# Loading the last fifth of the query weights through GpSimd, and finishing a head between the next products, in a one-token attention and ReGLU kernel

## The chip, the cores and the metric

The kernel runs on one core of a Trainium2 chip. The metric is device time in microseconds (us) of one execution, the median of several runs; lower is better. The core's engines are TensorE (PE in the profile; PEld are its weight loads), VectorE (DVE), ScalarE (ACT), GpSimd (POOL) and SyncE (SP). Sixteen DMA engines, which the core's queues share, bring data from the device's memory into the on-chip memory. A queue belongs to the engine that issues on it.

## The reference

One token `x` (640 values) goes through a layer norm, attention with 32 heads of 192 columns over a cache of 8192 positions, and a gated ReGLU block, with a residual sum after each. Everything is float32.

```python
def _A_ref(x, k_cache, v_cache, wq, wo):          # B = Sq = 1, D = 640, H = 32, Sk = 8192, Dh = 192
    q = (x @ wq).reshape(B, Sq, H, Dh).transpose(0, 2, 1, 3)
    scores = jnp.einsum("bhqd,bhkd->bhqk", q, k_cache) * (Dh ** -0.5)
    p = _softmax(scores, axis=-1)
    o = jnp.einsum("bhqk,bhkd->bhqd", p, v_cache)
    return o.transpose(0, 2, 1, 3).reshape(B, Sq, H * Dh) @ wo

def _B_ref(x, W_gate, W_up, W_down):              # F = 1536
    gate = jnp.einsum("bsd,df->bsf", x, W_gate)
    up = jnp.einsum("bsd,df->bsf", x, W_up)
    gate = gate * (gate > 0)
    return jnp.einsum("bsf,fd->bsd", gate * up, W_down)

h = x + _A_ref(_layernorm(x), A_k_cache, A_v_cache, A_wq, A_wo)
h2 = h + _B_ref(_layernorm(h), B_W_gate, B_W_up, B_W_down)
```

The two caches are 201 MB each, `wq` and `wo` 15.7 MB each, and the three matrices of the ReGLU block 3.9 MB each. Each value is used once.

## The kernel before

**Start.** ACT issues the load of `x` as the tile `xT` (L65: partition p holds the five values 5p to 5p+4, 20 bytes for each of 128 partitions) and once more as one row, `xrow` (L66). SP issues the query weights `wq` (L74) in three loads: two of 6144 KB, in which a partition gets two neighbouring rows (49,152 bytes in one piece), and one of 3072 KB with the fifth row of each partition. Each load fills one of the three buffers of the pool `kv`. VectorE and TensorE work out mean and variance of `xT` (L127 to L145) and write the normalized token `xn`. In between stand four small products on TensorE that add `xrow` to the accumulator `acc` (L150). Then come the products of `xn` and `wq` (L160), one weight row of a partition after the other, so buffer by buffer; each is 12 products, which the profile shows as 24 rows. ScalarE copies the result to `q4`, from which `query(h)` (L169) spreads one head's query over all partitions.

**Buffers set the order of the loads.** All key and value loads of SP (`load_kv`, L82; 6144 KB each) go through the same three buffers in turn. The first key load, K0, takes the buffer of the first `wq` load, so SP issues it when the products of the weight rows j = 0 and 1 are done; then SP issues `wo` of the first four heads (L91), K1 into the second buffer and V0 into the third. SP's instructions are in program order: whatever stands behind a waiting load waits too. After that the sequence is K2, V1, K3, V2 and so on, each load waiting until the third load before it has been used up.

**A head.** In `scores_and_softmax` VectorE multiplies the keys of head h+1 with the query in four parts (L187), GpSimd folds the two halves of each product (L188), and VectorE sums them to scores (L193). Between the four multiplications run the softmax steps of head h: the maximum (L198, L200, L203), the exponential on ScalarE (L205 to L210), the sum and its reciprocal (L212, L215). `values_of` then multiplies the probabilities of head h with its values, 32 products on TensorE (L229, 64 rows), and ScalarE scales the result into `ob` (L232).

**Finishing a head.** Once the scores of head h+1 are summed, `finish` treats the head before h: `to_columns` selects the result's diagonal by small products (L244) and VectorE transposes it into `oT` (L247); after the last head of a group of four (two for the last two groups), `output_of` multiplies `oT` by that group's `wo` into `acc` (L253).

**End.** The last value load comes in five parts. Then the ReGLU weights are loaded into the same buffers, the layer norm of `acc` is worked out, and products with up, gate and down weights (L327, L344) give the output.

`keep` fixes the order of the instructions that it wraps; the others are placed by the framework as they become ready.

Of the kernel before, what the change touches and what calls it, by code (L numbers as in the profile page):

```python
# [7 lines left out]
F32 = mybir.dt.float32  # L8
# [6 lines left out]
def kernel(  # L15
# [24 lines left out]
    QB = 512  # L40
    NQB = HPQ * DH // QB
    DG = D // NQ
    FG = F // NQ
# [18 lines left out]

    xT = const.tile([P, DJ], F32, name="xT")
    xrow = const.tile([1, D], F32, name="xrow")
    nc.scalar.dma_start(xT, x[0, 0].rearrange("(p j) -> p j", p=P))  # L65
    nc.scalar.dma_start(xrow, x[0])  # L66


    wq_v = wq.rearrange("(p j) n -> p j n", p=P)
    wq_ts = []  # L70
    for j in range(0, DJ, 2):
        n = min(2, DJ - j)
        t3 = kv.tile([P, 2 * TW], F32, name="kv_t").rearrange("p (j n) -> p j n", n=TW)[:, 0:n, :]
        nc.sync.dma_start(t3, wq_v[:, j:j + n, :])  # L74
# [98 lines left out]

    keep = tc.keep_in_program_order

    def scores_and_softmax(q, kt, sc_prev):


        steps = softmax_steps(sc_prev) if sc_prev is not None else iter(())
        sc = small.tile([P, NS], F32, name="sc") if kt is not None else None  # L180
        parts = []
        if kt is not None:
            k3 = kt.rearrange("p (r d) -> p r d", d=DH)
            parts = [(i0, k3[:, i0:i0 + SUB, :]) for i0 in range(0, NS, SUB)]
        res = None
        for i0, ks in parts:
            keep(nc.vector.tensor_mul(ks, ks, q[:, None, :].to_broadcast([P, SUB, DH])))  # L187
            nc.gpsimd.tensor_add(ks[:, :, 0:HD], ks[:, :, 0:HD], ks[:, :, HD:DH])  # L188
# [5 lines left out]
        return sc, res  # L194

    def softmax_steps(sc):
# [3 lines left out]
        nc.tensor.transpose(pt[0:1, 0:P], mp, ident)  # L200
        yield None
# [11 lines left out]
        yield None  # L213
        rl = small.tile([P, 1], F32, name="rl")
        keep(nc.vector.reciprocal(rl, pl[:, 0:1]))  # L215
        yield p, rl

# [7 lines left out]
    def values_of(h, p, rl, vt):  # L225
        po = pos[h % 2]
        for i in range(NP):
            g = i % NQ
            nc.tensor.matmul(po[g * Q:g * Q + 2, :], p[:, 2 * i:2 * i + 2],  # L229
                             vt[:, 2 * i * DH:(2 * i + 2) * DH], start=(i < NQ), stop=(i >= NP - NQ))  # L230
        ob = small.tile([P, 2 * DH], F32, name="ob")
        nc.scalar.activation(ob, po, AF.Copy, scale=rl)  # L232
        return ob

    def to_columns(h, ob, oT):

        gi, i = group_of[h]
        U = NQ // len(GROUPS[gi])
        W = DH // U
        pt = ps_s.tile([P, 512], F32, name="ps_small")  # L240
        for u in range(U):
            q0 = (i * U + u) * Q
            for k in range(2):
                nc.tensor.matmul(pt[q0:q0 + Q, 0:W], par[:, k, :], ob[:, k * DH + u * W:k * DH + (u + 1) * W],  # L244
                                 start=(k == 0), stop=(k == 1))
        s = slice(i * U * Q, (i + 1) * U * Q)
        keep(nc.vector.transpose(oT[s], pt[s, 0:W].rearrange("p (c j) -> p j c", c=Q)))  # L247

    def output_of(oT, wo_t, s, last):
        J = wo_t.shape[1]  # L250
        for j in range(J):
            for g in range(NQ):
                nc.tensor.matmul(acc[g * Q:(g + 1) * Q, :], oT[s, j, :], wo_t[s, j, g * DG:(g + 1) * DG],  # L253
                                 start=False, stop=(last and j == J - 1))

    def finish(h, ob, oT, wo_t):
        i, n = group_of[h][1], len(GROUPS[group_of[h][0]])
        to_columns(h, ob, oT)
        if n == 2 and h >= H - 2:
            output_of(oT, wo_t, slice(i * 64, (i + 1) * 64), h == H - 1)  # L260
        elif i == n - 1:
            output_of(oT, wo_t, slice(0, P), False)

    sc, _ = scores_and_softmax(query(0), load_kv(kf, 0, [2 * TW]), None)
    done = None
    for h in range(H):
        gi, i = group_of[h]
        if i == 0:
            wo_t = load_wo(gi)
            oT = small.tile([P, len(GROUPS[gi]) * DH // P, Q], F32, tag="oT", name="oT")  # L270
        more = h + 1 < H
        kt = load_kv(kf, h + 1, [2 * TW]) if more else None
        vt = load_kv(vf, h, [2 * TW] if more else [TW] + [TW // 4] * 4)
        sc, sm = scores_and_softmax(query(h + 1) if more else None, kt, sc)
        if done:
            finish(*done)
        done = h, values_of(h, *sm, vt), oT, wo_t
    finish(*done)


    sqd = row.tile([1, 1], F32, name="sqd")
# [94 lines left out]
```

## Time and profile before

| what | value |
|---|---|
| median of 3 runs | 1045.8 us (1045.74 to 1046.13) |
| the profiled execution | 1045.95 us |
| its span, first to last instruction | 1044.2 us |
| busy: PE, DVE, ACT, POOL | 39%, 64%, 4%, 42% of the span |
| read from device memory | 445.91 MB, 427 GB/s over the span |
| DMA busy in the first and last of 40 slices | 9 and 7 tenths, 394 and 296 GB/s |

A busy share is an average over stages with different limits. For this kernel the row of the DMA engines, the chain of work that ended last, and the timeline of the first 60 us and the last 60 us say the most. A load's time to landing counts from its issue, so it holds the time that it stands behind earlier loads in its queue.

### The profile page before, as it was taken

The numbers are of one execution on the slowest core, as the hardware profiler recorded it, in microseconds if no ns is written. First come the engines' busy times: TensorE is split into PE (matmuls) and PEld (weight loads), VectorE is DVE, ScalarE is ACT, GpSimd is POOL, SyncE is SP. The second block draws the span as 40 slices with busy tenths as digits, with TensorE's granted clock in tenths as the row PEclk, the third lists the DMA queues.
The fourth block names the chain that finished last, engine by engine and source line by source line (L and its number), as shares of the span: only waits on it lengthen the run. The fifth ranks groups of instructions, "written<-read, shape, count | busy, mean of one in ns | idle before, by whom it ended". The sixth has DMA issues, their size and how long they took to land.

```text
span 1044.2 us, 7373 instructions
## 1 busy us (share of the span) xinstructions
PE 408.9 (39%) x3136; PEld 151.6 (15%) x3136; DVE 664.1 (64%) x418; ACT 45.5 (4%) x140; POOL 438.6 (42%) x139
## 2 busy tenths in 40 slices
PE   1603343253442633354431533426232544424357
PEld 0101111020111211021110211112110211102123
DVE  1086777566667766467775666677664677766541
ACT  0000000000000000000000000000000000000010
POOL 0055555344455544245553444455542455554330
PEclk9856665666665666656665666656566666656668
DMA  9999999999999999999999999999999999999997
GB/s 394 443 435 426 424 443 431 427 430 441 427 432 430 437 430 422 435 437 433 430 430 433 437 430 430 431 433 430 432 426 441 432 429 436 431 432 423 435 422 296
DMA packets 13003, 446.39 MB, mean 428 GB/s; under 512 B 1573, under 2 KB 1577, under 8 KB 3114
## 3 DMA queue, kind: packets, MB, share of 16 engines
q1 hardware_dynamic: 12824, 445.92, 99.2%
q8 instruction: 24, 0.39, 0.2%
q14 instruction: 9, 0.07, 0.0%
q10 hardware_dynamic: 146, 0.01, 0.0%
HBM read 445.91 MB, written 0.00 MB: 427 GB/s over the span
## 4 chain that ended last, share of the span: by engine, by line
DMA 53%; DVE 26%; PE 16%; issue 3%; ACT 0%; ACTq 0%; DVEq 0%
DMA kv_t<-in_A_k_cache_dram 51%; DVE kv_t L187 20%; PE po L229 11%; DVE sc L193 5%; PE acc L253 3%; DMA xrow<-in_A_x_dram 2%; PE q L169 1%; PE qp L160 1%; PE pu L327 1%; DVE oT L247 0%; PE pd L344 0%; DVE m L203 0%; PE pg L327 0%; DVE rl L215 0%; DVE mp L198 0%
## 5 line engine op out<-in xcount | busy, mean ns | idle before, releaser
L188 POOL TENSOR_TENSOR kv_t<-kv_t 128x1536 f32<-128x1536 f32 x128 | 436.7, 3443 | 561.0 <-DVE mp L198 252.2
L187 DVE TENSOR_TENSOR kv_t<-kv_t,q 128x3072 f32<-128x3072 f32 x128 | 427.1, 3339 | 322.7 <-DMA kv_t<-in_A_k_cache_dram 313.0
L229 PE MATMUL po<-kv_t,p 128*2 128x384 f32 x2048 | 230.3, 596 | 10.7 <-DMA kv_t<-in_A_v_cache_dram 10.7
L193 DVE TENSOR_REDUCE sc<-kv_t 128x16 f32<-128x1536 f32 x128 | 214.8, 1732 | 0.0
L200 PE MATMUL ps_small<-ident,mp 128*1 128x128 f32 x32 | 11.1, 347 | 314.5 <-DVE mp L198 314.5
L229 PEld LDWEIGHTS po<-kv_t,p 128*2 128x2 f32 x2048 | 55.7, 97 | 167.5 <-issue 141.9
L169 PE MATMUL q<-q,sel 128*128 128x192 f32 x64 | 31.0, 589 | 118.2 <-DVE kv_t L187 118.2
L205 PE MATMUL ps_small<-m,ones 1*128 1x1 f32 x64 | 18.4, 355 | 96.5 <-DVE m L203 96.5
L200 PEld LDWEIGHTS ps_small<-ident,mp 128*1 128x1 f32 x32 | 2.5, 79 | 337.2 <-DVE mp L198 336.6
L244 PE MATMUL ps_small<-ob,par 128*32 128x192 f32 (+1 forms) x144 | 44.4, 479 | 0.7 <-ACT ob L232 0.7
L253 PE MATMUL acc<-wo_t,oT 128*32 128x160 f32 (+1 forms) x408 | 27.8, 453 | 37.5 <-DVE oT L247 37.5
L232 ACT ACTIVATE ob<-po,rl 128x384 f32<-128x384 f32 x32 | 18.6, 580 | 488.5 <-PE po L229 488.5
L169 PEld LDWEIGHTS q<-q,sel 128*128 128x128 f32 x64 | 15.7, 304 | 138.8 <-DVE kv_t L187 94.6
L205 PEld LDWEIGHTS ps_small<-m,ones 1*128 1x128 f32 x64 | 15.7, 303 | 105.0 <-DVE m L203 105.0
L212 PE MATMUL ps_small<-rs,ones 128*128 128x1 f32 x64 | 18.5, 359 | 24.8 <-ACT p L210 24.8
L253 PEld LDWEIGHTS acc<-wo_t,oT 128*32 128x32 f32 (+1 forms) x408 | 17.5, 162 | 54.5 <-DVE oT L247 49.2
L207 ACT ACTIVATE nb<-ps_small 128x1 f32<-128x1 f32 x32 | 5.5, 171 | 445.3 <-PE ps_small L205 445.3
L212 PEld LDWEIGHTS ps_small<-rs,ones 128*128 128x128 f32 x64 | 15.8, 307 | 27.5 <-ACT p L210 27.5
L160 PE MATMUL qp<-kv_t,xn 128*32 128x512 f32 x120 | 17.1, 726 | 5.0 <-DMA kv_t<-in_A_wq_dram 4.0
L244 PEld LDWEIGHTS ps_small<-ob,par 128*32 128x32 f32 x144 | 16.6, 152 | 9.9 <-ACT ob L232 1.4
L247 DVE STREAM_TRANSPOSE oT<-ps_small 32x192 f32<-32x192 f32 (+1 forms) x32 | 11.7, 364 | 8.8 <-PE ps_small L244 8.1
L203 DVE TENSOR_REDUCE m<-ps_small 1x1 f32<-1x128 f32 x32 | 8.7, 272 | 8.4 <-PE ps_small L200 8.4
(72 smaller groups left out, 75.0 us busy)
## 6 DMA issues: line engine op xcount, KB each, us to landing
kv_t<-in_A_k_cache_dram SPq DMA_DIRECT2D x32, 6144.0 KB, 36.3
kv_t<-in_A_v_cache_dram SPq DMA_DIRECT2D x31, 6144.0 KB, 23.4
wo_t<-in_A_wo_dram SPq DMA_DIRECT2D x7, 1920.0 KB, 27.5
kv_t<-in_A_wq_dram SPq DMA_DIRECT2D x2, 6144.0 KB, 18.0
ffn_a<-in_B_W_up_dram SPq DMA_DIRECT2D x1, 3840.0 KB
kv_t<-in_A_wq_dram SPq DMA_DIRECT2D x1, 3072.0 KB, 39.4
kv_t<-in_A_v_cache_dram SPq DMA_DIRECT2D x1, 3072.0 KB, 31.2
kv_t<-in_A_v_cache_dram SPq DMA_DIRECT2D x4, 768.0 KB, 34.8
```

The lines of the kernel that those rows point to most:

```text
L160: nc.tensor.matmul(qps[b][g * Q:(g + 1) * Q, :], xn[:, j:j + 1].to_broadcast([P, Q]), wq_ts[j][:, c0:c0 + QB], start=(j == 0), stop=(j == ...
L169: nc.tensor.matmul(q[:, 0:DH], sel[:, g, :], q4[:, i * DH:(i + 1) * DH], start=True, stop=True)
L187: keep(nc.vector.tensor_mul(ks, ks, q[:, None, :].to_broadcast([P, SUB, DH])))
L188: nc.gpsimd.tensor_add(ks[:, :, 0:HD], ks[:, :, 0:HD], ks[:, :, HD:DH])
L193: keep(nc.vector.reduce_sum(sc[:, i0:i0 + SUB], ks[:, :, 0:HD], axis=AX.X))
L200: nc.tensor.transpose(pt[0:1, 0:P], mp, ident)
L205: nc.tensor.matmul(pb[:, 0:1], ones[0:1, :], m1, start=True, stop=True)
L212: nc.tensor.matmul(pl[:, 0:1], ones, rs, start=True, stop=True)
L229: nc.tensor.matmul(po[g * Q:g * Q + 2, :], p[:, 2 * i:2 * i + 2], vt[:, 2 * i * DH:(2 * i + 2) * DH], start=(i < NQ), stop=(i >= NP - NQ))
L232: nc.scalar.activation(ob, po, AF.Copy, scale=rl)
L244: nc.tensor.matmul(pt[q0:q0 + Q, 0:W], par[:, k, :], ob[:, k * DH + u * W:k * DH + (u + 1) * W], start=(k == 0), stop=(k == 1))
L253: nc.tensor.matmul(acc[g * Q:(g + 1) * Q, :], oT[s, j, :], wo_t[s, j, g * DG:(g + 1) * DG], start=False, stop=(last and j == J - 1))
```

## The change

There are two edits. The first is in the loads at the start. The rows of `wq` are dealt out anew: partition p now holds rows 4p to 4p+3, in two loads of SP as before, and the last 128 rows (512 to 639) form the fifth row of the partitions in a rearranged order: partition 16a + b holds row 512 + 8b + a. That row is loaded by GpSimd in two transfers, columns 0 to 2175 and columns 2176 to 6143, each with a source whose outermost dimension is 8. `xT` has to hold the matching values of `x`, so its load is split into one of four values per partition (16 bytes) and one of a single value per partition (4 bytes), the second with the same rearranged source.

The second edit makes the finishing of a head a generator, `finish_steps`, whose steps run between the multiplications of the next head's keys (in `head_step`), like the softmax steps, and no longer after the sums of the scores.

```diff
+    CA = 2176
...
-    nc.scalar.dma_start(xT, x[0, 0].rearrange("(p j) -> p j", p=P))
+    JB = DJ - 1
+    nc.scalar.dma_start(xT[:, 0:JB], x[0, 0, 0:P * JB].rearrange("(p j) -> p j", p=P))
+    nc.scalar.dma_start(xT[:, JB:DJ], x[0, 0:1, P * JB:D].rearrange("o (b a) -> a b o", a=8))
     nc.scalar.dma_start(xrow, x[0])
-    wq_v = wq.rearrange("(p j) n -> p j n", p=P)
+    wq_v = wq[0:P * JB].rearrange("(p j) n -> p j n", p=P)
     wq_ts = []
-    for j in range(0, DJ, 2):
-        n = min(2, DJ - j)
-        t3 = kv.tile([P, 2 * TW], F32, name="kv_t").rearrange("p (j n) -> p j n", n=TW)[:, 0:n, :]
-        nc.sync.dma_start(t3, wq_v[:, j:j + n, :])
-        wq_ts += [t3[:, i, :] for i in range(n)]
+    for j in range(0, JB, 2):
+        t3 = kv.tile([P, 2 * TW], F32, name="kv_t").rearrange("p (j n) -> p j n", n=TW)
+        nc.sync.dma_start(t3, wq_v[:, j:j + 2, :])
+        wq_ts += [t3[:, i, :] for i in range(2)]
+    t = kv.tile([P, 2 * TW], F32, name="kv_t")[:, 0:TW]
+    wq_r = wq[P * JB:D].rearrange("(b a) n -> a b n", a=8)
+    for c0, c1 in ((0, CA), (CA, TW)):
+        nc.gpsimd.dma_start(t[:, c0:c1], wq_r[:, :, c0:c1])
+    wq_ts.append(t)
...
         for i0, ks in parts:
             keep(nc.vector.tensor_mul(ks, ks, q[:, None, :].to_broadcast([P, SUB, DH])))
             nc.gpsimd.tensor_add(ks[:, :, 0:HD], ks[:, :, 0:HD], ks[:, :, HD:DH])
-            res = next(steps, res)
-        for r in steps:
-            res = r
+            for w in works:
+                next(w, None)
...
-    def to_columns(h, ob, oT):
+    def finish_steps(h, ob, oT, wo_t):
...
                 nc.tensor.matmul(pt[q0:q0 + Q, 0:W], par[:, k, :], ob[:, k * DH + u * W:k * DH + (u + 1) * W],
                                  start=(k == 0), stop=(k == 1))
+        yield
         s = slice(i * U * Q, (i + 1) * U * Q)
         keep(nc.vector.transpose(oT[s], pt[s, 0:W].rearrange("p (c j) -> p j c", c=Q)))
-
-    def output_of(oT, wo_t, s, last):
+        yield
+        split = h >= H - 2
+        if not split and i < len(GROUPS[gi]) - 1:
+            return
+        if not split:
+            s = slice(0, P)
         J = wo_t.shape[1]
         for j in range(J):
             for g in range(NQ):
                 nc.tensor.matmul(acc[g * Q:(g + 1) * Q, :], oT[s, j, :], wo_t[s, j, g * DG:(g + 1) * DG],
-                                 start=False, stop=(last and j == J - 1))
+                                 start=False, stop=(h == H - 1 and j == J - 1))
+        yield
...
+        sm = []
+        soft = softmax_steps(sc, sm)
+        if h + 1 < H:
+            kt = load_kv(kf, h + 1, [2 * TW])
+            vt = load_kv(vf, h, [2 * TW])
+            sc = head_step(query(h + 1), kt, soft, done)
+        else:
+            vt = load_kv(vf, h, [TW] + [TW // 4] * 4)
+        for w in (soft, done):
+            for _ in w:
+                pass
+        done = finish_steps(h, values_of(h, *sm, vt), oT, wo_t)
```

The edits move instructions at three places. The first is the program's start. On ScalarE, whose queue loads `x` (`sdx` is a step of the first layer norm), there stood before:

```order
L65 DMA xT<-in_A_x_dram 128x5
L66 DMA xrow<-in_A_x_dram 1x640
L117 ACT_TABLE_LOAD
L117 ACTIVATE sdx<-var,eps 128x1
L164 COPY q_212<-qp_149 128x512
```

and on the same engine stands now:

```order
L69 DMA xT<-in_A_x_dram 128x4
L70 DMA xT<-in_A_x_dram 128x1x1
L71 DMA xrow<-in_A_x_dram 1x640
L126 ACT_TABLE_LOAD
L126 ACTIVATE sdx<-var,eps 128x1
```

The load of one value for each of 128 partitions has come between `xT` and `xrow`. The second place is SP's queue at the start, where the kernel before issues all of `wq` ahead of the first cache loads:

```order
L74 DMA kv_t<-in_A_wq_dram 128x12288 x2
L74 DMA kv_t<-in_A_wq_dram 128x6144
L82 DMA kv_t<-in_A_k_cache_dram 128x12288
L91 DMA wo_t<-in_A_wo_dram 128x3840
L82 DMA kv_t<-in_A_k_cache_dram 128x12288
L82 DMA kv_t<-in_A_v_cache_dram 128x12288
```

In the changed kernel SP keeps the two large loads alone, and GpSimd issues the rest behind its constants (`ident`, `sel`) and ahead of its first work on a head:

```order
masks.py:199 AFFINE_SELECT ident<-ident 128x128
L114 MEMSET sel 1x128 x4
L83 DMA kv_t<-in_A_wq_dram 128x1x2176
L83 DMA kv_t<-in_A_wq_dram 128x1x3968
L193 TENSOR_TENSOR kv_t<-kv_t 128x16x96 x128
```

What follows on SP's queue is the same sequence as before, one load shorter ahead of it. The third place is TensorE and VectorE in the last heads, at the step that multiplies the keys of head 31, runs the softmax of head 30 and finishes head 29. On TensorE before (`m_2665` is that softmax's maximum, `po` the sum of the values' products):

```order
L200 MATMUL ps_small<-ident,mp 1x128
L205 MATMUL ps_small<-m_2665,ones 128x1
L212 MATMUL ps_small<-rs,ones 128x1
L244 MATMUL ps_small<-ob,par 32x96 x4
L229 MATMUL po_216<-kv_t,p 2x384
L253 MATMUL acc<-wo_t,oT 32x160 x12
L229 MATMUL po_216<-kv_t,p 2x384 x31
```

and on the same engine, at the same step, now:

```order
L204 MATMUL ps_small<-ident,mp 1x128
L249 MATMUL ps_small<-ob,par 32x96 x4
L209 MATMUL ps_small<-m_2672,ones 128x1
L263 MATMUL acc<-wo_t,oT 32x160 x5
L216 MATMUL ps_small<-rs,ones 128x1
L263 MATMUL acc<-wo_t,oT 32x160 x7
L234 MATMUL po_218<-kv_t,p 2x384 x32
```

The products with `wo` have moved from behind the first of the 32 value products of head 30 to ahead of them all. On VectorE the same step read before:

```order
L187 TENSOR_TENSOR kv_t<-kv_t,q 128x3072
L203 TENSOR_REDUCE m_2665<-ps_small 1x1
L187 TENSOR_TENSOR kv_t<-kv_t,q 128x3072
L215 RECIPROCAL rl<-ps_small 128x1
L187 TENSOR_TENSOR kv_t<-kv_t,q 128x3072
L193 TENSOR_REDUCE sc<-kv_t 128x16 x4
L247 STREAM_TRANSPOSE oT<-ps_small 64x96
```

and reads now:

```order
L192 TENSOR_TENSOR kv_t<-kv_t,q 128x3072
L207 TENSOR_REDUCE m_2672<-ps_small 1x1
L253 STREAM_TRANSPOSE oT<-ps_small 64x96
L192 TENSOR_TENSOR kv_t<-kv_t,q 128x3072
L219 RECIPROCAL rl<-ps_small 128x1
L192 TENSOR_TENSOR kv_t<-kv_t,q 128x3072
L197 TENSOR_REDUCE sc<-kv_t 128x16 x4
```

The transposition has moved from behind the four sums of the scores to behind the second multiplication; the other heads but the first and the last have moved in the same way.

More of the change, by code (lines that the diff above doesn't have):

```diff
@@ L174, with head_step @@
     keep = tc.keep_in_program_order
[L176 to L185, printed above, removed]
+    def head_step(q, kt, *works):
+        sc = small.tile([P, NS], F32, name="sc")
+        k3 = kt.rearrange("p (r d) -> p r d", d=DH)
+        parts = [(i0, k3[:, i0:i0 + SUB, :]) for i0 in range(0, NS, SUB)]
         for i0, ks in parts:
@@ L199, in softmax_steps @@
         pt = ps_s.tile([P, 512], F32, name="ps_small")
-        nc.tensor.transpose(pt[0:1, 0:P], mp, ident)
-        yield None
+        keep(nc.tensor.transpose(pt[0:1, 0:P], mp, ident))
+        yield
         m1 = small.tile([1, 1], F32, name="m1")
@@ L245, in to_columns @@
                                  start=(k == 0), stop=(k == 1))
+        yield
         s = slice(i * U * Q, (i + 1) * U * Q)
         keep(nc.vector.transpose(oT[s], pt[s, 0:W].rearrange("p (c j) -> p j c", c=Q)))
-    def output_of(oT, wo_t, s, last):
+        yield
+        split = h >= H - 2
[3 more added lines that the diff above has]
+            s = slice(0, P)
         J = wo_t.shape[1]
@@ L253, in output_of @@
                 nc.tensor.matmul(acc[g * Q:(g + 1) * Q, :], oT[s, j, :], wo_t[s, j, g * DG:(g + 1) * DG],
-                                 start=False, stop=(last and j == J - 1))
[L256 to L265, printed above, removed]
+                                 start=False, stop=(h == H - 1 and j == J - 1))
+        yield
+    sc = head_step(query(0), load_kv(kf, 0, [2 * TW]))
+    done = iter(())
     for h in range(H):
@@ L270 @@
             oT = small.tile([P, len(GROUPS[gi]) * DH // P, Q], F32, tag="oT", name="oT")
[L271 to L278, printed above, removed]
+        sm = []
[10 more added lines that the diff above has]
+        done = finish_steps(h, values_of(h, *sm, vt), oT, wo_t)
+    for _ in done:
+        pass
     sqd = row.tile([1, 1], F32, name="sqd")
```

7 lines of the change are left out of this document (3 added, 4 removed).

## The prediction

> **What bounds the kernel now.** I read first the profile's page: the DMA row of its 40 slices, the queues and the chain of work that ended last. Then a table of DMA share and throughput by stage, the chain of the first 100 us in order of time, and the timeline of both ends. From the page:
>
> ```profile
> span 1044.2 us, 7373 instructions
> ...
> DMA  9999999999999999999999999999999999999997
> ...
> q1 hardware_dynamic: 12824, 445.92, 99.2%
> ...
> q10 hardware_dynamic: 146, 0.01, 0.0%
> ```
>
> The DMA engines are busy in every slice but the last. The profiled execution took 1045.95 us, of which 1.75 lie around the span. By stage (start, length, busy time of PE, PEld, DVE, ACT and POOL, granted clock, DMA share, GB/s):
>
> ```profile
> 2.00:18.00 16.00, 0.00 (x0) 0.00 (x0) 0.00 (x0) 1.04 (x1) 0.52 (x3) 1.00 0.97 409
> ...
> 56.00:1003.00 947.00, 356.58 (x2601) 131.62 (x2601) 654.61 (x378) 37.68 (x124) 436.67 (x128) 0.62 1.00 432
> ...
> 1034.00:1036.00 2.00, 1.78 (x24) 0.48 (x16) 0.06 (x1) 0.00 (x0) 0.00 (x0) 1.00 0.70 282
> 1036.00:1038.00 2.00, 0.57 (x17) 0.55 (x21) 1.34 (x2) 0.00 (x0) 0.00 (x0) 1.00 0.53 205
> 1038.00:1039.00 1.00, 1.00 (x40) 0.96 (x32) 0.00 (x0) 0.00 (x0) 0.00 (x0) 1.00 0.38 146
> 1039.00:1040.00 1.00, 1.00 (x36) 0.96 (x32) 0.00 (x0) 0.00 (x0) 0.00 (x0) 1.00 0.11 41
> 1040.00:1042.00 2.00, 0.90 (x28) 0.55 (x20) 0.38 (x1) 0.00 (x0) 0.00 (x0) 1.00 0.00 0
> ```
>
> For 947 us the share is 1.00 at 432 GB/s, so 27.0 KB per us and engine: no compute step there costs time. What is left is the two ends. In the last 6 us the engines do not stop together: idle are 0.30 x 2 + 0.47 x 2 + 0.62 + 0.89 = 3.05 us of engine time on average. The first end is a chain:
>
> ```profile
> 1.19 20.24 DMA xrow<-in_A_x_dram
> 21.42 0.04 issue
> 21.47 0.73 PE acc L150 x2
> ...
> 24.42 7.34 PE qp L160 x48
> 31.76 0.02 issue
> 31.77 23.80 DMA kv_t<-in_A_k_cache_dram
> ```
>
> The load of `x` gates the normalized token, this the 48 rows of products of the first `wq` buffer, and their end the issue of the first key load K0 at 31.77. K0 lands at 55.57. That is harmless before, because the engines still work on `wq` when K0 is queued: they need the second 6144 KB load to 33.3 (next part) and the 3072 KB load behind it, 3,145,728 B / 16 / 27.0 KB = 7.3 us more. So K0's issue has a margin of 33.3 + 7.3 - 31.8, some 9 us, less what it takes to start a load.
>
> **The change part by part. First, the split load of `x`.** The issues of the first 24 us, and the timeline there:
>
> ```profile
> q10 hardware_dynamic: 146, 0.01, 0.4%
> issues: line engine op xcount, KB each, median us to landing
> kv_t<-in_A_wq_dram SPq DMA_DIRECT2D x2, 6144.0 KB, 18.0
> kv_t<-in_A_wq_dram SPq DMA_DIRECT2D x1, 3072.0 KB, 39.4
> xT<-in_A_x_dram ACTq DMA_DIRECT2D x1, 2.5 KB, 18.2
> ```
> ```profile
> 0.75 1.34 SPq L74 DMA_DIRECT2D kv_t<-in_A_wq_dram  x3
> ...
> 18.93 0.16 DVE L127 TENSOR_REDUCE s<-xT 128x1 f32<-128x5 f32 x1 [17.05 <-DMA xT<-in_A_x_dram]
> ...
> 20.42 0.16 DVE L137 TENSOR_REDUCE s<-xsq 128x1 f32<-128x5 f32 x1
> ...
> 22.13 0.58 PE L139 MATMUL ps_small<-s,ones 128*128 128x1 f32 x2
> ...
> 33.32 5.36 PE L160 MATMUL qp<-kv_t,xn 128*32 128x512 f32 x48 [1.62 <-DMA kv_t<-in_A_wq_dram]
> ...
> 59.19 13.63 POOL L188 TENSOR_TENSOR kv_t<-kv_t 128x1536 f32<-128x1536 f32 x4 [56.57 <-DVE kv_t L187]
> ```
>
> 2.5 KB of `xT` take 18.2 us, as long as the 6144 KB of the first `wq` load, 18.0. The packet count of ACT's queue says why: 146 = 128 rows of 20 bytes, one packet for `xrow`, and 17 that signal the ends (16 engines and one). So each row is a packet of its own, eight on each engine; the first `wq` load is 128 pieces of 49,152 bytes, eight on each engine too. Both end together: an engine takes one packet of `x`, then one of `wq`, in turn, and a `wq` packet lasts 49,152 / 27.0 KB = 1.8 us.
>
> The change makes this queue longer. Eight rows of 16 bytes per engine are followed by the single column: 128 pieces of 4 bytes, which the source's outermost dimension of 8 should put on eight engines, 16 on each. That is 24 turns, and SP has only 16 large packets per engine to take turns with (two loads). So the column is through only when both `wq` loads are, seen at 33.3 in the row of L160. On all 16 engines it would be 8 + 8 = 16 turns: the same end. GpSimd's packets take their turns in between. I take the small transfer for the same eight engines: 16 rows x 2176 x 4 = 139,264 B, 5.2 us. `xT` is then complete at 33.3 + 5.2 = **38.5 us** instead of 18.9.
>
> From there to K0's issue the kernel before takes 31.77 - 18.93 = 12.84 us. Of this 22.13 - 20.58 = 1.55 goes, since TensorE stood behind the wait for `xrow` (the row at 21.47), and `xrow` now comes right behind the column on queues that are empty. K0 is issued at 38.5 + 12.84 - 1.55 = **49.8**. Behind it on SP wait `wo`, K1 and V0, and on TensorE all products of `wq`, so no other load can fill in: the eight engines run dry at about 38, the other eight at 33.3 + 16 x 3968 x 4 / 27.0 KB = 42.7.
>
> On idle engines a 6144 KB load lands 18.0 us after its issue (the first `wq` load), so K0 lands at 67.8. The shift against 55.57 is **12.2 us**. If the 18.0 holds a start-up that does not come again, K0 needs 6,291,456 B / 432 GB/s = 14.6 and a start of some 1 us (SP issues first at 0.75, and the share is 0.97 from 2.00 on): landing at 65.4, a shift of 9.9. I take 12.2, the row measured with empty queues. After K0 nothing has slack to give it back: at a share of 1.00 each later load moves by as much.
>
> **Second, the unequal shares.** GpSimd's transfers give eight engines 139,264 B each and the other eight 253,952 B, a difference of 114,688 B or 4.2 us. Against an even split the late engines at the end would finish 2.1 us earlier. But all engines run dry before K0, at 38 and 42.7 against 49.8: the head start is waited out, and worth 0. No row shows what GpSimd pays for issuing; between 0 and 1 us each costs nothing, since it stands idle up to its first sum at 59 us, and the last fifth of `wq` is needed only some 5.4 us after 49.8 (the 48 rows at 33.32).
>
> **Third, the finishing of a head.**
>
> ```profile
> L247 DVE STREAM_TRANSPOSE oT<-ps_small 32x192 f32<-32x192 f32 (+1 forms) x32 | 11.7, 364 | 8.8 <-PE ps_small L244 8.1
> ...
> kv_t<-in_A_v_cache_dram SPq DMA_DIRECT2D x31, 6144.0 KB, 23.4
> ```
> ```profile
> 1003.62 1.83 PE L253 MATMUL acc<-wo_t,oT 128*32 128x160 f32 x24 [4.55 <-DVE oT L247]
> 1005.23 6.71 PE L229 MATMUL po<-kv_t,p 128*2 128x384 f32 x62
> ...
> 1037.43 3.47 PE L344 MATMUL pd<-ffn_b,guT 128*32 128x160 f32 x96 [1.64 <-DVE guT L339]
> ```
>
> In the steady part a transposition of 0.36 us moves ahead of the score sums, so the key buffer comes free that much later. What hides it: a value load is issued 23.4 us before it lands and needs 14.6 to move, so it stands 8.8 us in the queue. Without that cover it would cost 0.36 per head, 11 us in all. TensorE no longer waits 4.55 us for `oT` in front of head 30's value products, and the last head starts about 6 us earlier. But the down weights still arrive until just before 1040 (the share of 0.11 and then 0.00), and the last products end at 1040.90. So at most 0.9 us can be gained; it could be lost again if TensorE, waiting for data, ran slower. I take **-0.4**, near the middle.
>
> The sum: 1045.95 + 12.2 + 0 - 0.4 = 1057.75, against this execution; the median shown is 0.15 lower, and I say **1057.7**.
>
> The Trainium skill, in "DMA: Bandwidth & Descriptors", section "Queues, rings and completion order", says that each engine goes round the rows that have work and drains one packet before it switches. The 18.2 us of `xT` beside the 18.0 of `wq` agree. The same section calls 9 to 17 descriptors a typical packet; the 146 packets disagree for rows of 20 bytes, and the measurement decides. By the typical figure the whole of `x` would take two or three turns, and the sum would be that of the first rival.
>
> **The rivals.** *The small pieces travel together.* Pieces of 16 and 4 bytes are not what this trace shows (20 bytes), and if an engine took eight or more in one packet, `xT` would be there after a few turns of 1.8 us, well before 18.9. The products then wait for the first `wq` load only (18.8), K0 is issued at about 26.3, long before the engines run dry, and the unequal shares reach the end of the program. If the smaller share falls on the engines that end last, 2.1 us go: 1043.8, faster. For it speaks the uneven end (3.05 us of idle); against it the 146 packets.
>
> *The shares are not what they should be.* If GpSimd spreads both transfers over all 16 engines, each gets 7.3 us instead of 5.2, and `xT` lands 2.1 later: 1059.8. If the larger share falls on the eight engines with the column, 9.4: 1061.9. The Trainium skill, same page, section "Why a DMA increments its semaphore by 16 and not by 1", gives the largest count up to 16 that divides both sides' outermost sizes, here 8 of 8 and 128, but reports GpSimd copies that went to all 16; no run here shows either. With pieces that travel together besides, an even split is 1045.9, no change, and shares on the wrong halves give +2.1, 1048.
>
> *GpSimd starts late.* If its transfers come to the engines only after 33 us, the column does not wait for them: 5.2 less, 1052.5.
>
> **How the numbers follow.** Forecast 0.68; other shares with the column queueing 0.07; GpSimd late 0.06; pieces together and right shares (faster) 0.13; pieces together and even shares (no change) 0.03; pieces together and wrong shares (slower) 0.03. Slower by over 0.2%, which is about what a measurement of this kernel can tell from no change (2.1 us): 0.68 + 0.07 + 0.06 + 0.03 = 0.84; within it 0.03; faster 0.13. The range takes in the late start (1052.5), the lower shift (9.9 with the whole 0.9: 1054.9) and the larger share (1061.9): 1052 to 1062.5, which holds 0.81 and leaves the three cases of pieces together out.
>
> **What would show it.** Right: the first reduction of `xT` waits to 37 to 39 us, K0 is issued near 50, the DMA row has a hole of about 10 us in its second slice, and from the first key products on each step stands 10 to 12 us later with a share of 1.00; the engines still stop unevenly at the end. Wrong: `xT` lands before 20 us and the DMA row has no hole (first rival); a landing at 42 or 33 says which shares or which start. The finishing is right if the products with `wo` no longer wait for `oT` near the end and the last products wait for the down weights instead.

## The result, and the profile after

The changed kernel takes **1072.9 us** (median of 4 runs, 1072.0 to 1074.1) against 1045.8 before (1045.7 to 1046.1): a ratio of 1.026, with an interval of 1.0245 to 1.0270. It is slower by 27 us, where the prediction said 12; the time lies outside its range. The profiled execution took 1074.12 us, 28.2 more than that of before; it is the slowest of the four.

The rows of the page, as before:

```profile
span 1072.3 us, 7410 instructions
...
DMA  9969999999999999999999999999999999999997
GB/s 329 231 259 429 436 437 430 435 430 427 431 440 424 437 429 431 430 433 433 436 426 436 428 435 429 435 426 436 431 435 430 433 431 431 435 428 429 438 419 291
...
q1 hardware_dynamic: 12680, 442.77, 96.9%
q0 software_dynamic: 544, 3.15, 1.4%
...
q10 hardware_dynamic: 282, 0.01, 0.0%
```

Only the first three slices of 26.8 us differ. A hole in the DMA row is there, but it is small (a 6 in the third slice). The row of throughput below it is the one to read: with engines shown as busy in 9 tenths of the second slice, they move 231 GB/s. In this view a busy engine is one that has a packet open, whatever the rate at which it moves data.

By stage (start, length, busy time of PE, PEld, DVE, ACT and POOL, granted clock, DMA share, GB/s):

```profile
4.00:20.00 16.00, 0.00 (x0) 0.00 (x0) 0.00 (x0) 0.02 (x1) 0.00 (x0) 1.00 1.05 375
20.00:39.00 19.00, 0.00 (x0) 0.00 (x0) 0.00 (x0) 0.00 (x0) 0.00 (x0) 1.00 0.96 308
39.00:52.00 13.00, 0.00 (x0) 0.00 (x0) 0.00 (x0) 0.00 (x0) 0.00 (x0) 1.00 1.00 168
52.00:61.00 9.00, 6.28 (x32) 2.35 (x36) 2.46 (x16) 0.29 (x1) 0.00 (x0) 1.00 0.46 102
61.00:66.00 5.00, 5.00 (x44) 1.28 (x40) 0.00 (x0) 0.00 (x0) 0.00 (x0) 1.00 0.00 0
...
84.00:1031.00 947.00, 360.46 (x2679) 133.59 (x2683) 656.41 (x379) 37.68 (x124) 438.21 (x128) 0.62 1.00 432
```

From 84 us on there is no difference: 432 GB/s, as before. In front of it stand 13 us at a share of 1.00 and 168 GB/s, 9 us at a share of 0.46 and 102 GB/s, and the 5 us of the forecast's hole, in which nothing moves. The timeline of the start, and K0 in the chain of waits:

```profile
53.27 0.16 DVE L136 TENSOR_REDUCE s<-xT 128x1 f32<-128x5 f32 x1 [51.38 <-DMA xT<-in_A_x_dram]
...
57.24 15.51 PE L169 MATMUL qp<-kv_t,xn 128*32 128x512 f32 x120 [1.00 <-DVE par L118]
65.10 0.33 SPq L91 DMA_DIRECT2D kv_t<-in_A_k_cache_dram  x1
83.20 3.35 DVE L192 TENSOR_TENSOR kv_t<-kv_t,q 128x3072 f32<-128x3072 f32 x1 [25.66 <-DMA kv_t<-in_A_k_cache_dram]
```
```profile
65.10 17.98 DMA kv_t<-in_A_k_cache_dram
```

`xT` was seen at 53.27 (18.93 before, 38.5 forecast), K0 was issued at 65.10 (31.77 before), and landed at 83.08. Before, it landed at 55.57, so the start lost 27.5 us: nearly the whole loss, as the forecast's mechanism has it, but more than twice its size.

The 282 packets of `q10` are 128 rows of four values, 128 single values, one for `xrow`, and 25 ends: 16 engines, 8 engines and one. So the column did go to eight engines, with a turn for each value. What remained to be explained was 38.5 against 53.27. The DMA view of the changed kernel, from 20 to 39 us (queue, packets, MB, share of the 16 engines' time):

```profile
q1 hardware_dynamic: 122, 5.36, 86.5%
q0 software_dynamic: 121, 0.49, 8.9%
```

and the same view from 44 to 48 and from 48 to 52 us:

```profile
q1 hardware_dynamic: 8, 0.39, 58.7%
...
q0 software_dynamic: 123, 0.46, 68.1%
q10 hardware_dynamic: 61, 0.00, 1.8%
q1 hardware_dynamic: 8, 0.00, 0.4%
```

In the first stretch the `wq` packets of SP's queue `q1` move 5.36 MB / (0.865 x 16 x 19 us) = 20.4 KB per us and engine, where the forecast had 27.0 throughout. The view counts a packet where it starts. The last eight large ones (0.39 MB) start before 48 us and move 0.39 MB / (0.587 x 16 x 4) = 10.4 KB per us and engine, so each takes 4.7 us; the eight small packets of `q1` in the last stretch can be read as their end signals, and by narrower views all eight start between 50 and 52 us. The second `wq` load thus ends near 50, some 17 us later than the 33.3 of before. Only behind it do ACT's last pieces come through (61 start in these 4 us, 51 of them between 51 and 52), and GpSimd's queue `q0` moves its data at 0.46 MB / (0.681 x 16 x 4) = 10.6 KB per us and engine.

Nor did the packets of both GpSimd transfers "take their turns in between" from the start, as the forecast had it: in the trace no row of the larger one (15,872 bytes) starts before 39 us. SP's packets are at their slowest from then on, when both transfers run.

### The profile page after: what moved, and what is told of

The parts are those of the page before. It is cut to its first block, busy times and chain, and to the rows that moved or that the text cites. A ratio compares the mean times of both kernels' runs of the same rounds, so it can differ in the third digit from the quotient of the medians.

```text
span 1072.3 us, 7410 instructions
## 1 busy us (share of the span) xinstructions
PE 405.0 (38%) x3136; PEld 150.9 (14%) x3136; DVE 666.0 (62%) x418; ACT 45.5 (4%) x140; POOL 441.4 (41%) x141
## 3 DMA queue, kind: packets, MB, share of 16 engines
q0 software_dynamic: 544, 3.15, 1.4%
## 4 chain that ended last, share of the span: by engine, by line
DMA 61%; DVE 19%; PE 12%; another core or an unknown queue 5%; issue 3%; SPq 0%; ACT 0%; DVEq 0%
DMA kv_t<-in_A_k_cache_dram 51%; DVE kv_t L192 16%; PE po L234 9%; DMA kv_t<-in_A_v_cache_dram 8%; DMA ffn_b<-in_B_W_down_dram 3%; DVE sc L197 2%; PE q L178 1%; PE qp L169 1%; DVE oT L253 0%; PE pd L353 0%; DVE m L207 0%; DVE rl L219 0%; DVE mp L202 0%; DVE po L227 0%
## 5 line engine op out<-in xcount | busy, mean ns | idle before, releaser
L234 PE MATMUL po<-kv_t,p 128*2 128x384 f32 x2048 | 222.3, 597 | 10.0 <-DMA kv_t<-in_A_v_cache_dram 10.0
L263 PE MATMUL acc<-wo_t,oT 128*32 128x160 f32 (+1 forms) x408 | 33.1, 447 | 0.4 <-DVE oT L253 0.4
L216 PEld LDWEIGHTS ps_small<-rs,ones 128*128 128x128 f32 x64 | 15.8, 307 | 24.9 <-ACT p L214 24.9
```

## The experiments

Three theories for the slow rate were set against each other: **P**, the destination (eight engines write neighbouring partitions in step and meet in the on-chip memory); **S**, the source (rows that lie eight apart in device memory); **G**, GpSimd's path as such. Beside them stood the question how much of the loss is the column's queue alone. Each kernel is told by its difference from the changed kernel, and ratios are to the kernel before.

**1. The finishing alone** (start of before), **and the start alone** (finishing of before).

```diff
 e1_finish_only
-    for c0, c1 in ((0, CA), (CA, TW)):
-        nc.gpsimd.dma_start(t[:, c0:c1], wq_r[:, :, c0:c1])
+    for j in range(0, DJ, 2):
+        nc.sync.dma_start(t3, wq_v[:, j:j + n, :])
...
 e2_start_only
-            sc = head_step(query(h + 1), kt, soft, done)
+        sc, sm = scores_and_softmax(query(h + 1) if more else None, kt, sc)
+        if done:
+            finish(*done)
...
```

> The start of the kernel before with the new finishing of a head alone. My forecast's third term, corrected by the trace of the changed kernel: the steady part costs nothing (the DMA share stays 1.00), head 30's value products no longer wait 4.55 us for oT, and the last head starts some 7 us earlier; then the last products wait for the down weights. By the forecast -0.4 us (1045.4). Rival: TensorE, which waits for data, runs at half the granted clock in the last products (0.50 in the changed kernel's window 1066 to 1068), and the time goes up by 0.3 to 1 us (1046.1 to 1046.8). Second rival: the steady part suffers too, by 0.36 us a head, and the time is some 1057.

> The new start alone, with the finishing of a head as before. If the two edits do not meet, the loss is all here: 1072 to 1073.5. In the changed kernel's profile TensorE waited for the down weights at half the granted clock and the end came 0.6 us later than the shift of K0; with the old finishing that wait should be gone and the time 0.3 to 0.8 us below the changed kernel's 1072.9, if it can be told from the scatter of that kernel (1072.0 to 1074.1). Rival: the new finishing and the new start work against each other, and the start alone costs much less than 27 us.

The finishing alone took 1045.99 us, ratio 1.0000 (0.9991 to 1.0009); the start alone 1073.0, 1.0260 (1.0246 to 1.0274), the time of the whole change. So all of the loss is the start's. Two smaller expectations were missed: the finishing alone gained nothing (1045.4 was forecast, and 1046.1 or more if the clock were halved), and the start alone is not 0.3 to 0.8 us below the changed kernel. In the profiles, the last head's value products before

```profile
1015.98 5.33 PE L229 MATMUL po<-kv_t,p 128*2 128x384 f32 x62
```

and with the finishing alone the same products, and the last ones with the down weights:

```profile
1009.54 6.46 PE L226 MATMUL po<-kv_t,p 128*2 128x384 f32 x62
...
1034.08 1.02 PE L345 MATMUL pd<-ffn_b,guT 128*32 128x160 f32 x24 [1.64 <-DVE guT L340]
1035.60 1.74 PE L345 MATMUL pd<-ffn_b,guT 128*32 128x160 f32 x24 [0.50 <-DMA ffn_b<-in_B_W_down_dram]
1037.92 2.15 PE L345 MATMUL pd<-ffn_b,guT 128*32 128x160 f32 x40 [0.58 <-DMA ffn_b<-in_B_W_down_dram]
1040.34 0.48 PE L345 MATMUL pd<-ffn_b,guT 128*32 128x160 f32 x8 [0.27 <-DMA ffn_b<-in_B_W_down_dram]
```

The value products end at 1016.0 instead of 1021.3, the last products begin at 1034.08 instead of 1037.43, and they end at 1040.82 instead of 1040.90. The wait of 4.55 us for `oT` is gone, and TensorE waits for the down weights in its place, up to the last eight rows: 5.3 us earlier inside, 0.1 at the end.

**2. `x` ahead of `wq`.** Both loads of `xT` go to SP's queue, ahead of the two `wq` loads; the GpSimd transfers stay.

```diff
-    nc.scalar.dma_start(xT[:, 0:JB], ...)
-    nc.scalar.dma_start(xT[:, JB:DJ], ...)
+    nc.sync.dma_start(xT[:, 0:JB], ...)
+    nc.sync.dma_start(xT[:, JB:DJ], ...)
```

> The changed kernel, with the two loads of xT issued by SP ahead of wq, so that their small packets take no turns with large ones. Column theory (the forecast's): the queue of small packets is what costs, xT lands before 6 us, K0 is issued near 31 us, the DMA engines never run dry, and of the 27 us only 1 to 2 remain (1045 to 1048: SP's two issues ahead of wq cost some 1.6, the shares may give 2.1 back). Transfer theory: the two GpSimd transfers on eight engines each are slow themselves (168 GB/s from 39 to 52 us, 102 from 52 to 61), and take engine time from whatever runs beside them: the mean engine was through at 56.5 us instead of 39.2, so up to 17 us stay, 1055 to 1064, though no engine is idle and K0 is issued near 31.

1080.9 us, ratio 1.0331 (1.0317 to 1.0345): slower than the changed kernel, and outside what either theory expected. Yet `xT` was there at 3.96 us, and up to 80 us the engines were never idle (shares of 0.98 to 1.02). Windows and timeline of this kernel:

```profile
4.00:20.00 16.00, 1.85 (x10) 1.19 (x10) 2.43 (x16) 0.30 (x1) 0.00 (x0) 1.00 0.98 344
20.00:40.00 20.00, 7.59 (x48) 2.06 (x48) 0.00 (x0) 0.00 (x0) 0.00 (x0) 0.93 0.98 323
40.00:60.00 20.00, 8.76 (x52) 2.05 (x52) 0.00 (x0) 0.00 (x0) 0.00 (x0) 0.64 1.00 296
60.00:80.00 20.00, 0.00 (x0) 0.00 (x0) 0.00 (x0) 0.00 (x0) 0.00 (x0) 0.53 1.02 248
129.00:135.00 6.00, 6.00 (x56) 1.50 (x52) 6.00 (x4) 0.00 (x0) 1.49 (x1) 0.67 0.54 180
```
```profile
33.63 0.33 SPq L91 DMA_DIRECT2D kv_t<-in_A_k_cache_dram  x1
...
88.72 4.36 PE L169 MATMUL qp<-kv_t,xn 128*32 128x512 f32 x20 [30.72 <-DMA kv_t<-in_A_wq_dram]
93.13 0.33 SPq L91 DMA_DIRECT2D kv_t<-in_A_v_cache_dram  x1
```

With the column out of the way, the slow transfers stayed slow, and took the key loads with them: from 4 to 80 us the engines are busy and move 344, 323, 296 and 248 GB/s. Against 432 that is 16 x 88 + 20 x 109 + 20 x 136 + 20 x 184 = 9,990 KB too few, or 23 us of the 35 lost. GpSimd's packets now take turns with K0 and K1, the last products of `wq` wait for them until 88.7, V0 is issued at 93.1, and later the engines run dry for some us (129 to 135: a share of 0.54). So the slow rate is a loss of its own. In the changed kernel it runs while the column is queueing and before K0 is issued, and the two together cost 27 us; beside the key loads the slow rate alone costs 35.

**3. One GpSimd transfer on all 16 engines.** `x` on SP as in 2, natural order of the rows.

```diff
+    nc.sync.dma_start(xT[:, JB:DJ], x[0, 0:1, P * JB:D].rearrange("o p -> p o"))
-    for c0, c1 in ((0, CA), (CA, TW)):
-        nc.gpsimd.dma_start(t[:, c0:c1], wq_r[:, :, c0:c1])
+    nc.gpsimd.dma_start(t, wq[P * JB:D])
```

> As e3_x_first, but the last 128 rows of wq come in their natural order in one GpSimd transfer of 3072 KB whose outermost size is 128 on both sides, so on all 16 engines; the column of xT accordingly. Theory G (a transfer that GpSimd issues is slow whatever its layout): the same loss as in e3_x_first. Theories P (eight engines write neighbouring partitions in step and meet on few entrances of the on-chip memory) and S (source rows that lie eight rows apart): the loss is gone, 1046 to 1048.

1046.13 us, ratio 0.9998 (0.9988 to 1.0007), and from 20 to 39 us

```profile
20.00:39.00 19.00, 8.04 (x48) 2.16 (x48) 0.00 (x0) 0.00 (x0) 0.00 (x0) 0.97 1.01 436
```

GpSimd's path moves the same 3072 KB at the full rate: **G falls**.

**4. Eight engines, other partitions.** `x` on SP; four GpSimd transfers, each to 32 partitions, the source's outermost dimension still 8 and its rows still eight apart. In such a transfer an engine writes 4 neighbouring partitions, not 16.

```diff
+    for g in (0, 2, 1, 3):
+        r0 = P * JB + 32 * g
+        nc.gpsimd.dma_start(t[32 * g:32 * g + 32, :], wq[r0:r0 + 32].rearrange("(b a) n -> a b n", a=8))
```

> As e3_x_first, with sources of outermost size 8 and rows eight apart as in the changed kernel, but in four GpSimd transfers to 32 partitions each (0-31, 64-95, 32-63, 96-127), all columns, so that an engine writes four neighbouring partitions and the eight of one transfer 32 different ones. The Trainium skill's page 'SBUF - State Buffer' (Door 1: The DMA port swizzle) has four neighbouring partitions on one of 16 ports, so that here each engine of a transfer has a port to itself, where in the changed kernel two engines of a transfer share one, four with both transfers. Theory P: the loss is gone, 1046 to 1049 (four more issues on SP). Theory S: as slow as e3_x_first. Theory G: as slow as e3_x_first and e4_even16.

1049.2 us, ratio 1.0031 (1.0019 to 1.0043). Its windows:

```profile
20.00:39.00 19.00, 7.57 (x48) 2.01 (x48) 0.00 (x0) 0.00 (x0) 0.00 (x0) 1.00 0.99 427
39.00:52.00 13.00, 7.63 (x60) 2.02 (x64) 0.00 (x0) 0.00 (x0) 0.00 (x0) 0.74 1.01 436
```

The full rate, with eight engines to a transfer and rows eight apart: S falls as well, and P holds. The 3.3 us left fit SP's issues: it issues five small loads ahead of `wq`, whose first issue is at 4.22 instead of 0.75 (experiment 8, with two small loads there, loses 0.9).

**5. Neighbouring rows, old partitions.** As in 2, but an engine's rows are neighbours in device memory. The fifth row of a partition is then another row of `wq` than the reference's, so the queries differ.

```diff
-    wq_r = wq[P * JB:D].rearrange("(b a) n -> a b n", a=8)
+    wq_r = wq[0:144].rearrange("(a r) n -> a r n", r=18)[:, 0:16]
```

> As e3_x_first, but the two GpSimd transfers read rows that lie next to each other (engine a rows 18a to 18a + 15 of wq) instead of rows eight apart; engines and destinations stay as they are. The fifth row of each partition is thus another row of wq than the reference's, so the queries differ. Theory P (destination): as slow as e3_x_first, 1075 to 1085. Theory S (rows apart): the loss goes, 1046 to 1049.

1081.4 us, ratio 1.0331 (1.0294 to 1.0368), the time of experiment 2, with the same rates (323 GB/s from 20 to 40 us, 251 from 60 to 80). The order of the source makes no difference.

**6. In between.** Two transfers to 64 partitions each: an engine writes 8 neighbouring partitions. `x` on SP.

```diff
+    for g in range(2):
+        r0 = P * JB + 64 * g
+        nc.gpsimd.dma_start(t[64 * g:64 * g + 64, :], wq[r0:r0 + 64].rearrange("(b a) n -> a b n", a=8))
```

> As e5_own_ports, but in two transfers to 64 partitions each (0-63 and 64-127), so that an engine writes eight neighbouring partitions; by the port map two engines of a transfer then meet on a port at a time, as in the changed kernel, but the two transfers keep to different halves. Theory P: a loss between e5_own_ports and e3_x_first, 1052 to 1070. Rival (a transfer to fewer partitions, or in pieces of 24,576 bytes, is fast for another reason than its ports): as e5_own_ports, 1047 to 1049.

1062.0 us, ratio 1.0146 (1.0121 to 1.0171), and 292 and 299 GB/s:

```profile
20.00:39.00 19.00, 4.95 (x24) 1.35 (x28) 0.00 (x0) 0.00 (x0) 0.00 (x0) 1.00 1.02 292
39.00:52.00 13.00, 3.00 (x28) 0.76 (x20) 0.00 (x0) 0.00 (x0) 0.00 (x0) 0.78 0.94 299
```

The loss grows with the number of neighbours that an engine writes: 4, 8 and 16 give +3.3 (SP's issues), +15.8 and +35 us with `x` loaded first. Two other things change along with it. The number of transfers falls from 4 to 2, but the kernel with 16 neighbours has 2 as well. The pieces are 24,576 bytes here and in experiment 4, and 8,704 and 15,872 bytes, unequally shared, with 16 neighbours; experiment 9 has unequal shares and pieces of 17,408 bytes at the full rate.

**7. The column alone, and the column's queue at the full rate.** First without GpSimd: the fifth row of `wq` by SP, the column on ACT. Then the changed kernel with its loads of `x` on ACT and the transfers of experiment 4.

```diff
 e6_column_only
+    nc.scalar.dma_start(xT[:, JB:DJ], x[0, 0:1, P * JB:D].rearrange("o p -> p o"))
+    nc.sync.dma_start(t, wq[P * JB:D])
 e7_column_queue
+    nc.scalar.dma_start(xT[32 * g:32 * g + 32, JB:DJ], ...)
+    nc.gpsimd.dma_start(t[32 * g:32 * g + 32, :], wq[r0:r0 + 32].rearrange("(b a) n -> a b n", a=8))
```

> No GpSimd transfer: SP loads the last 128 rows of wq in natural order as a third load, and ACT loads xT as in the change, four values and then one value per partition (128 pieces of 4 bytes, here on all 16 engines). Turn theory: 8 + 8 packets of x per engine must take turns with 16 large ones of wq, so xT is there at 33 us, when the second wq load is; by the 11.83 us that the changed kernel took from xT to K0's issue (53.27 to 65.10), K0 is issued at 45, lands at 63 instead of 55.6, and the time is +7.5, 1053.4. Rival (small pieces travel together, or only the eight-engine layout delays them): xT lands before 20 us, no idle engines, 1045.9.

> The changed kernel with its loads of x on ACT's queue, but the GpSimd transfers of e5_own_ports (32 partitions each, in which an engine keeps to four neighbouring partitions). It asks whether my forecast's sum holds once the transfers run at the full rate. Each engine gets 7.3 us of them instead of 5.2, so xT is complete at 33.3 + 7.3 = 40.6, K0 is issued at 52.4, lands at 70.4, and the time is +14.8, 1060.7. Rival (the single column is what makes the engines slow, by its 4-byte pieces or by its eight engines): xT lands after 50 us as in the changed kernel, and the time is 1070 to 1075.

The column alone: 1053.2 us, ratio 1.0064 (1.0046 to 1.0082), where 1053.4 was expected. `xT` lands behind both `wq` loads, and K0 comes late:

```profile
33.49 0.16 DVE L134 TENSOR_REDUCE s<-xT 128x1 f32<-128x5 f32 x1 [31.61 <-DMA xT<-in_A_x_dram]
45.03 0.33 SPq L89 DMA_DIRECT2D kv_t<-in_A_k_cache_dram  x1
```

With GpSimd's data at the full rate: 1060.55 us, ratio 1.0134 (1.0108 to 1.0160), where 1060.7 was expected, and

```profile
41.01 0.16 DVE L138 TENSOR_REDUCE s<-xT 128x1 f32<-128x5 f32 x1 [39.13 <-DMA xT<-in_A_x_dram]
52.19 0.33 SPq L93 DMA_DIRECT2D kv_t<-in_A_k_cache_dram  x1
69.96 13.15 DVE L194 TENSOR_TENSOR kv_t<-kv_t,q 128x3072 f32<-128x3072 f32 x4 [24.98 <-DMA kv_t<-in_A_k_cache_dram]
```

Its DMA view from 20 to 39 us, beside that of the changed kernel above:

```profile
q1 hardware_dynamic: 136, 5.90, 71.8%
q0 software_dynamic: 169, 1.97, 24.7%
```

SP's packets move 5.90 MB / (0.718 x 16 x 19) = 27.0 KB per us and engine, GpSimd's 26.2. So between experiment 7 and the changed kernel, which differ in which partitions a transfer writes (and so in the number of transfers and of loads for the column), lie 41.01 against 53.27 for `xT`, and 12 of the 27 us.

**8. A version without the losses.** Transfers as in experiment 4 with even shares, `x` in two loads on SP, the new finishing.

```diff
+    nc.sync.dma_start(xT[:, JB:DJ], x[0, 0:1, P * JB:D].rearrange("o (b a) -> a b o", a=32))
+    wq_r = wq[P * JB:D].rearrange("(b a) n -> a b n", a=32)
+    for g in (0, 2, 1, 3):
+        nc.gpsimd.dma_start(t[32 * g:32 * g + 32, :], wq_r[8 * g:8 * g + 8])
```

> The changed kernel, finishing included, without collisions and without the queue of small packets: xT is loaded by SP ahead of wq in two loads, and GpSimd's transfers go to 32 partitions each (0-31, 64-95, 32-63, 96-127), so by the port map to eight ports each, with even shares. Base for the next two. Expected 1046 to 1047.5: the before, with SP's two issues (1.3 us) ahead of wq.

1046.9 us, ratio 1.0004 (0.9996 to 1.0013): the whole loss is gone, and nothing is gained.

**9. Unequal shares.** From experiment 8, 1792 columns of one half's partitions go over to the engines of the other half (M = 1792, TW = 6144; first half less in the one, second half less in the other).

```diff
 e11_less_second
+    ((0, 0, TW), (2, M, TW), (1, 8, TW), (3, M, TW), (2, 0, M), (1, 0, 4), (3, 0, M), (1, 4, 8))
 e12_less_first
+    ((0, M, TW), (2, 8, TW), (1, M, TW), (3, 0, TW), (2, 0, 4), (0, 0, M), (2, 4, 8), (1, 0, M))
```

> As e10_even, but 1792 columns of the partitions 64 to 127 go to the eight engines of the odd transfers (the ones that wrote partitions 0 to 63), so that the two halves of the engines differ by 114,688 B each (4.2 us), as in the change; four transfers of a few columns keep the alternation. Share theory (the forecast's first rival: unequal shares bring the late engines forward by 2.1 us): one of e11 and e12 is 2 us faster than e10_even, 1044 to 1045, and the other 2 us slower, 1048 to 1049. Port theory: a port's bytes are what they were, the columns that change engines meet the other half's packets on its ports, and both are as e10_even or up to 3 us slower.

> As e11_less_second the other way round: 1792 columns of the partitions 0 to 63 go to the engines of the even transfers. Share theory: 2 us faster than e10_even if e11 is 2 us slower, or the reverse. Port theory: both as e10_even or up to 3 us slower.

1056.4 us, ratio 1.0101 (1.0085 to 1.0116), and 1058.3, 1.0118 (1.0104 to 1.0131). Both are slower than either theory expected. In the first of the two the rate is full at first, with pieces of (6144 - 1792) x 4 = 17,408 bytes to 32 partitions:

```profile
20.00:39.00 19.00, 8.22 (x48) 2.16 (x48) 0.00 (x0) 0.00 (x0) 0.00 (x0) 0.91 1.03 446
...
63.63 4.74 PE L170 MATMUL qp<-kv_t,xn 128*32 128x512 f32 x24 [14.88 <-DMA kv_t<-in_A_wq_dram]
68.42 0.33 SPq L92 DMA_DIRECT2D kv_t<-in_A_v_cache_dram  x1
```

So neither shorter pieces nor unequal shares alone make a transfer slow. But the pieces that were moved over are issued last and take turns with K0's packets, the last products of `wq` wait for them until 63.6, and V0 is issued at 68.4, where experiment 8 issues it at 51.3. Whether unequal shares could pay is therefore **left open**: no run here had them without a late piece.

## Why the prediction was right or wrong

- **The queue of small pieces (right).** Each value of the column took a turn, and the column came through only behind both `wq` loads: 51 of ACT's packets start between 51 and 52 us, behind the last large `wq` packets. Experiment 7 has it alone: 33.49 us, where the forecast put the end of both loads at 33.3. The rival in which the pieces travel together falls.
- **The term 5.2 us in 33.3 + 5.2 = 38.5 (wrong; this is the step that failed).** It let GpSimd's 139,264 B per engine pass at 27.0 KB per us, and SP's packets keep that rate beside them. Measured, `xT` came at 33.3 + 20.0. SP's packets fell to 20.4 KB per us and at the end to 10.4, and were through near 50; GpSimd's fell to 10.6. With transfers to 32 partitions, where an engine carries 7.3 us of GpSimd's data instead of 5.2, the term is 41.01 - 33.3 = 7.7, and the kernel takes 1060.55 us; the forecast's own sum for a share of 7.3 is 1059.8, so the rest of the sum holds. The rate came from a steady part in which every engine takes part in every load; that eight engines which write 16 neighbouring partitions each would move data as fast was not shown by any row, and the forecast bounded the shares only, not the rate.
- **From `xT` to K0's issue (right).** Forecast 11.29, measured 65.10 - 53.27 = 11.83. Half a us more in TensorE's products for the first buffer, which the chain of waits gives 7.83 us, against 7.34 before.
- **K0 lands 18.0 us after its issue (right).** 17.98 in the chain; the lower value, 15.6, falls.
- **The shift of 12.2 (mechanism right, size off).** 27.5 measured; the difference of 15.3 is 14.8 from `xT` and 0.5 from the products. That nothing gives it back after K0 held: 947 us at a share of 1.00.
- **Unequal shares worth 0 here (held).** All engines ran dry ahead of K0 (0 GB/s from 61 to 66 us). Part of the engines was through near 52 and the rest at 61 (the mean share of 0.46 between fits eight of 16), so the times of 38 and 42.7 failed with the same term.
- **The finishing, -0.4 (0 to -0.9): mechanism right, size off.** Steady part: nothing, as said, by the ratio of 1.0000 and 432 GB/s. End: the wait for `oT` went and the wait for the down weights took its place, as said. But the bound of 0.9 let the last products end when the weights' last bytes arrive, just before 1040. With the finishing alone the last eight rows still wait for their weights until 1040.34 and end at 1040.82, so 0.1 was all there was to gain, less than the times can show (0.9991 to 1.0009). In the changed kernel's profile the last products end 1069.03 - 1040.90 = 28.1 later, 0.6 more than the start's 27.5. Its end:

```profile
1061.33 1.02 PE L353 MATMUL pd<-ffn_b,guT 128*32 128x160 f32 x24 [1.64 <-DVE guT L348]
1063.29 1.02 PE L353 MATMUL pd<-ffn_b,guT 128*32 128x160 f32 x24 [0.94 <-DMA ffn_b<-in_B_W_down_dram]
1065.63 3.40 PE L353 MATMUL pd<-ffn_b,guT 128*32 128x160 f32 x48 [1.32 <-DMA ffn_b<-in_B_W_down_dram]
```
```profile
1066.00:1067.00 1.00, 1.00 (x24) 0.77 (x20) 0.00 (x0) 0.00 (x0) 0.00 (x0) 0.50 0.25 97
1067.00:1068.00 1.00, 1.00 (x21) 0.77 (x16) 0.00 (x0) 0.00 (x0) 0.00 (x0) 0.50 0.03 13
```

  TensorE waits three times, and the clock that it is granted falls to 0.50 just when the last 48 rows run: 3.40 us, where 1.02 for 24 would make 2.04. Not all of these 1.4 us are lost, presumably because the last rows would have waited for data in any case; the end shows 0.6. The forecast named this loss ("lost again if TensorE, waiting for data, ran slower") and gave it no price. In the profile of the start alone the clock stays at 1.00, and the loss is absent: K0 lands at 82.25, 26.7 later than before, and the last products end at 1067.69, 26.8 later.

```profile
1066.00:1067.00 1.00, 0.90 (x28) 0.46 (x20) 0.00 (x0) 0.00 (x0) 0.00 (x0) 1.00 0.10 38
...
1067.21 0.48 PE L353 MATMUL pd<-ffn_b,guT 128*32 128x160 f32 x8 [0.31 <-DMA ffn_b<-in_B_W_down_dram]
```

  The medians of the two kernels (1073.0 and 1072.9) do not tell them apart.

What P is in the chip is argued, not shown: no row names a part of the on-chip memory. The Trainium skill, "SBUF — State Buffer", section "Door 1: The DMA port swizzle (why `[64,N]` ≈ `[32,N]`)", says that four neighbouring partitions share one of 16 ports, and that a copy to partitions 0 to 15 reaches four ports and was measured at 104 GB/s. Engines that write 16 neighbours each, in step, reach four at a time; the 102 GB/s from 52 to 61 us agree, and by the same rule engines that write 4 neighbours each have a port of their own, as the 427 GB/s of experiment 4 have it. By that page's 104 GB/s, GpSimd's 3.15 MB are an estimate of 30 us, an upper end that the forecast lacked; measured, they were through at 61, which is 27.7 behind the 33.3 of `wq` alone.

## What to carry to other kernels

A transfer's price is a rate on certain engines to certain partitions: before a load is split so that fewer engines carry it, look at which partitions each of them then writes, and take the steady part's rate only for transfers of the steady part's shape. Read throughput beside the busy share: at a share of 1.00 these engines moved 168 GB/s. Tiny loads that gate a chain belong ahead of the large loads on the same queue, since each of their pieces takes a turn, but that pays only if nothing behind them is slow, and each such load delays the large ones by its issue.

## What the runs showed of the hardware that was not expected

- Transfers on eight engines that write 16 neighbouring partitions each slow the loads beside them, too: from 20 to 39 us SP's packets ran at 20.4 KB per us and engine in the changed kernel, at 27.0 with transfers to 32 partitions.
- Loading `x` first, a cure for the queue, made the kernel slower (1080.9 against 1072.9 us), because the slow transfers then ran beside the key loads.
- GpSimd's queue shows 544 packets: 256 rows of data, 32 ends (16 for each transfer), and 256 more. One reading is a small packet per row on the engines that take no part, which takes its turn there as well, so that the second transfer waits behind the first one's small packets on its own eight engines. It would explain why the larger transfer starts only at 39 us; no run tested it.
- TensorE's granted clock was 0.50 from 1066 us on in the changed kernel, after waits of 1.64, 0.94 and 1.32 us, and 0.50 from 1036 to 1039 us with the finishing alone, after waits of 1.64 and 0.50. With the start alone it stayed at 1.00, with waits of 1.64 and 0.31. What decides between them was not tested.
